# Five small loads put ahead on ScalarE's queue in a linear attention with two MLPs

## The chip, the cores and the metric

One core of a Trainium2 chip runs the whole program. Its engines are TensorE (PE in the profile; its weight loads are PEld), VectorE (DVE), ScalarE (ACT), GpSimd (POOL) and SyncE (SP), which here only issues DMAs. The metric is the device time of one launch in microseconds; the time of a kernel is the median of its runs.

## The reference

Attention without a softmax, an RMS norm over each head, and two MLPs one after the other, all in float32:

```python
kv = np.einsum('bhsd,bhse->bhde', k, v)
out = np.einsum('bhsd,bhde->bhse', q, kv)                    # 4 batches, 8 heads, 576 rows, 64 wide
out = out / np.sqrt(np.mean(out * out, axis=-1, keepdims=True) + 1e-06) * g_norm
x = out.transpose(0, 2, 1, 3).reshape(2304, 512)
h = x @ moe_w_in                                             # 512 -> 2048
x = (np.maximum(h, 0.0) + np.log1p(np.exp(-np.abs(h)))) @ moe_w_out    # softplus, 2048 -> 512
h = x @ moe2_w_in
result = np.maximum(0.01 * h, h) @ moe2_w_out                # leaky ReLU
```

In the kernel q, k, v are 4.7 MB each; the weights are named w1 to w4 and come as 8.4 MB each, since each number is stored in two words.

## The kernel before

The work falls into two stages. In the **attention stage** (about the first 70 us) 16 units of one batch and two heads each go through a pipeline: the sync queue loads q, k and v of a unit (`load`, tiles qa, ka, va, 128 partitions with four rows each; five buffers of each), and once per batch the 64 rows of each head that are left over (qr, kr, vr). The tiles are copied into another order (qp, kp) by ScalarE, VectorE or GpSimd (`copy_to`, line 418 on ScalarE), TensorE transposes q (line 497), multiplies k by v (lines 506 and 511) and q by the result (line 547), VectorE and ScalarE take squares, sums and the norm, and TensorE transposes the normed rows (tile xn, line 632) into xy, which stays on the chip. Beside that, the first weights are loaded (tile mf, line 667) and decoded.

In the **MLP stage** TensorE multiplies in blocks of 128x128 by 384 or 256 columns: line 922 for the first product of an MLP, lines 1179 and 1184 for the second, which read the tile rb. rb is laid over the attention's tiles when these are done with. Intermediate blocks go to a scratch tensor xscr in DRAM and come back.

What stands in which order is settled before the program runs: `Plan` collects the steps, takes the first 500 or so from a list written out by hand (`FIRST`, where S is a load on the sync queue, A ScalarE, D VectorE, P GpSimd, E TensorE) and orders the rest by due times. `keep_warm` (line 476) puts multiplications of idle data on TensorE, 17 calls at the start (`N_WARM`) and a few in between, each of two instructions in the trace. The first thing on ScalarE is the load of its table (line 1395), the last line before `plan.run()`.

A DMA reports its end through one of eight semaphores, named DMAHW0 to DMAHW7, which are handed out in turn over all the DMAs of the program, whichever queue they stand on. A DMA whose semaphore is still in use by the one eight places ahead waits for that one.

Of the kernel before, what the change touches and what calls it, by code (L numbers as in the profile page):

```python
# [168 lines left out]
def linear_attention_two_mlps(  # L169
# [32 lines left out]
    nc = tc.nc  # L202
# [34 lines left out]
    const = ctx.enter_context(tc.tile_pool(name="const", bufs=1))  # L237
# [155 lines left out]
        nc.gpsimd.memset(t_[RL:], 0.0)  # L393
    for t_ in qtl:
        nc.gpsimd.memset(t_[:, RL:2 * RL], 0.0)

    plan = Plan()
    op = plan.op
# [872 lines left out]
    for t in range(2):  # L1271
# [3 lines left out]
                out=graw[t * D:(t + 1) * D, :], in_=g_norm.rearrange("(p o) -> p o", o=1)  # L1275
# [116 lines left out]
                w2_decode(g + 1, no - 4)  # L1392
    with tc.manual_schedule():

        nc.scalar.preload_act_table_set("natural_log_exp_and_others")
        plan.run()

# [31 lines left out]
```

## Time and profile before

| | us |
|---|---|
| median of 3 runs | 779.09 (778.41 to 779.94) |
| the profiled execution | 778.38 |
| its span, from first to last instruction | 776.5 |
| TensorE busy | 770.4 |
| VectorE busy | 676.3 |
| ScalarE busy | 546.4 |

The profile shows one execution. Busy time says how full an engine is, but TensorE's ends are modelled, so a little waiting can hide in it. The chain of waits tells which work ended last at each moment, followed back from the end; "SPq" in it is time in which the sync queue issues a DMA, and "DMA" the time from issue to landing. The windows show busy time, DMA share and GB/s in each stretch, which is where a start-up shows. Times in the trace count from the start of the span.

### The profile page before, as it was taken

The numbers are of one execution on the slowest core, as the hardware profiler recorded it, in microseconds if no ns is written. First come the engines' busy times: TensorE is split into PE (matmuls) and PEld (weight loads), VectorE is DVE, ScalarE is ACT, GpSimd is POOL, SyncE is SP. The second block draws the span as 40 slices with busy tenths as digits, with TensorE's granted clock in tenths as the row PEclk, the third lists the DMA queues.
The fourth block names the chain that finished last, engine by engine and source line by source line (L and its number), as shares of the span: only waits on it lengthen the run. The fifth ranks groups of instructions, "written<-read, shape, count | busy, mean of one in ns | idle before, by whom it ended". The sixth has DMA issues, their size and how long they took to land.

```text
span 776.5 us, 13282 instructions
## 1 busy us (share of the span) xinstructions
PE 770.4 (99%) x5061; PEld 767.0 (99%) x5061; DVE 676.3 (87%) x1079; ACT 546.4 (70%) x936; POOL 20.0 (3%) x36
## 2 busy tenths in 40 slices
PE   9999999999999999999999999999999999999998
PEld 9999999999999999999999999999999999999997
DVE  3999999999899887996899999998799877886667
ACT  4899989886776865863688799977667645554441
POOL 2430000000000000000000000000000000000000
PEclk9999999999999999999999999999999999999999
DMA  9986767694794784683675659786675772562814
GB/s 282 324 290 211 289 235 290 240 336 166 308 336 147 277 343 135 254 310 124 239 290 203 264 202 345 286 306 225 257 274 178 281 252 104 215 240 99 312 42 122
DMA packets 77103, 186.99 MB, mean 241 GB/s; under 512 B 11504, under 2 KB 51440, under 8 KB 77040
## 3 DMA queue, kind: packets, MB, share of 16 engines
q1 hardware_dynamic: 75424, 185.36, 66.6%
q10 hardware_dynamic: 1616, 0.79, 0.4%
q8 instruction: 40, 0.66, 0.3%
q14 instruction: 23, 0.19, 0.1%
HBM read 146.80 MB, written 39.32 MB: 240 GB/s over the span
## 4 chain that ended last, share of the span: by engine, by line
PE 95%; DVE 2%; SPq 1%; ACT 1%; DMA 1%; issue 1%; DVEq 0%; ACTq 0%
PE ps L922 43%; PE ps L1179 23%; PE ps L1184 23%; PE ps L1012 2%; PE ps L547 1%; PE ps L506 1%; DMA ka<-in_k_dram 1%; SPq L447 1%; PE ps L632 1%; DVE ss L573 0%; PE ps L497 0%; PE ps L554 0%; DVE xn L610 0%; ACT sq L568 0%; PE ps L511 0%
## 5 line engine op out<-in xcount | busy, mean ns | idle before, releaser
L922 PE MATMUL ps<-ra 128*128 128x384 f32 x1932 | 386.1, 335 | 0.0
L922 PEld LDWEIGHTS ps<-ra 128*128 128x128 f32 x1932 | 332.1, 188 | 0.0
L1179 PE MATMUL ps<-rb 128*128 128x256 f32 x1512 | 204.4, 282 | 0.0
L1184 PE MATMUL ps<-rb 128*128 128x384 f32 x1008 | 201.2, 334 | 0.0
L1179 PEld LDWEIGHTS ps<-rb 128*128 128x128 f32 x1512 | 198.4, 189 | 0.1
L1184 PEld LDWEIGHTS ps<-rb 128*128 128x128 f32 x1008 | 177.1, 188 | 0.0
L951 ACT ACTIVATE rb<-mf 128x768 fp32r<-128x768 f32 x154 | 130.0, 845 | 63.1 <-PE ps L1179 34.0
L956 DVE TENSOR_TENSOR rb<-mf,rb 128x768 fp32r<-128x768 f32 x154 | 146.5, 952 | 23.4 <-ACT rb L951 22.8
L794 DVE TENSOR_TENSOR xy<-ps,xy 128x384 f32<-128x384 f32 (+2 forms) x247 | 134.4, 548 | 33.8 <-PE ps L1179 22.8
L1036 DVE TENSOR_TENSOR mf<-mf 128x768 f32<-128x768 f32 x68 | 64.2, 951 | 2.4 <-ACT mf L937 1.5
L1229 ACT ACTIVATE mf<-ps 128x384 f32<-128x384 f32 x92 | 44.9, 488 | 29.0 <-PE ps L922 28.5
L1236 DVE TENSOR_TENSOR mf<-ps,mf 128x384 f32<-128x384 f32 x92 | 50.5, 553 | 12.3 <-PE ps L922 8.4
L1241 ACT ACTIVATE ps<-ps 128x384 f32<-128x384 f32 x46 | 22.1, 481 | 20.3 <-PE ps L922 20.1
L937 ACT ACTIVATE mf<-mf 128x768 f32<-128x768 f32 x26 | 21.8, 843 | 15.1 <-DVE mf L1236 14.9
L1098 ACT ACTIVATE rb<-rc 128x512 fp32r<-128x512 f32 x44 | 27.5, 625 | 3.5 <-PE ps L1179 2.7
L1101 DVE TENSOR_TENSOR rb<-rc,rb 128x512 fp32r<-128x512 f32 x44 | 29.8, 682 | 0.2 <-ACT rb L1098 0.2
L943 ACT ACTIVATE mf<-mf 128x768 f32<-128x768 f32 x24 | 20.2, 840 | 11.0 <-DVE mf L1236 11.0
L1195 ACT ACTIVATE ps<-ps 128x384 f32<-128x384 f32 (+2 forms) x44 | 21.1, 480 | 6.3 <-PE ps L1184 3.1
L943 ACT ACTIVATE mf<-ps 128x384 f32<-128x384 f32 x32 | 15.6, 488 | 10.4 <-PE ps L922 10.2
L789 ACT ACTIVATE xy<-ps 128x384 f32<-128x384 f32 (+2 forms) x40 | 19.0, 483 | 3.2 <-PE ps L1179 1.5
L707 ACT ACTIVATE sqr<-mf 128x512 uint16<-128x512 uint16 x26 | 20.4, 784 | 0.0
L825 ACT ACTIVATE ra<-xy 128x768 fp32r<-128x768 f32 x21 | 17.7, 841 | 3.7 <-PE ps L922 3.4
(125 smaller groups left out, 754.9 us busy)
## 6 DMA issues: line engine op xcount, KB each, us to landing
ra<-xscr SPq DMA_DIRECT2D x124, 768.0 KB, 6.2
xscr<-ra SPq DMA_DIRECT2D x37, 768.0 KB, 4.2
mf<-in_moe_w_in_dram SPq DMA_DIRECT2D x18, 512.0 KB, 5.5
mf<-in_moe_w_out_dram SPq DMA_DIRECT2D x18, 512.0 KB, 5.0
lf<-in_moe_w_in_dram SPq DMA_DIRECT2D x14, 512.0 KB, 7.3
lf<-in_moe_w_out_dram SPq DMA_DIRECT2D x14, 512.0 KB, 4.9
ka<-in_k_dram SPq DMA_DIRECT2D x16, 256.0 KB, 5.3
qa<-in_q_dram SPq DMA_DIRECT2D x16, 256.0 KB, 5.4
```

What stands on the lines that cost most here:

```text
L794: {"D": t_d(n)}, lambda e: nc.vector.tensor_tensor(dst, src, dst, ALU.add),
L922: nc.tensor.matmul(o, w_[:, a, c:c + P], e_[:, b, kk, :], start=(not on and which < 2 and kk == 0 and n == 0), stop=(kk == 1 and n == 2), ...
L943: lambda e: nc.scalar.activation(dst(), src(), AF.Prelu, alpha=0.01),
L951: {"A": t_a(n)}, lambda e: nc.scalar.activation(g[:, 0, :, :], c.ap, AF.Copy),
L956: lambda e: nc.vector.tensor_tensor(g[:, 1, :, :], c.ap, g[:, 0, :, :].bitcast(F32), ALU.subtract),
L1036: lambda e: nc.vector.tensor_tensor(to.ap, x.ap, y.ap, ALU.subtract),
L1098: op({"A": t_a(512)}, lambda e: nc.scalar.activation(w_[:, 0], src(), AF.Copy), sk, hk)
L1101: lambda e: nc.vector.tensor_tensor(w_[:, 1], src(), w_[:, 0].bitcast(F32), ALU.subtract), sk + hk, lk,
L1179: nc.tensor.matmul(y[:, 256 * (j % 2):256 * (j % 2 + 1)], G_[:, a, m, js], w_[:, b, m, :], **flags)
L1184: nc.tensor.matmul(y[:, :BN], w_[:, a, m, js], G_[:, b, m, :], **flags)
L1229: {"A": t_a(BN)}, lambda e: nc.scalar.activation(c[:, m, :], src, AF.Copy),
L1236: lambda e: nc.vector.tensor_tensor(c[:, m, :], src, c[:, m, :], ALU.add),
```

## The change

Ahead of all other work of ScalarE, its queue issues five DMAs, one each for q, k, v, w1 and w2. Each fetches 80 single words: from five places, a fifth of the tensor apart, 16 words with 64 bytes between them, one word for each of 16 partitions. They land in five tiles of 16x5 words that nothing reads. The tiles are taken from the pool `const`, ahead of the attention's tiles.

```diff
--- before.py
+++ after.py
@@ -393,6 +393,13 @@
         nc.gpsimd.memset(t_[RL:], 0.0)
     for t_ in qtl:
         nc.gpsimd.memset(t_[:, RL:2 * RL], 0.0)
+
+    first_words = []
+    for t_, name in ((q, "q"), (k, "k"), (v, "v"), (w1, "w1"), (w2, "w2"),):
+        w = t_.rearrange("b h s d -> (b h s d)") if len(t_.shape) == 4 else t_.rearrange("a b -> (a b)")
+        step = w.shape[0] // 5
+        w = w[:5 * step].rearrange("(n m) -> n m", m=step)[:, :256].rearrange("n (r x) -> r n x", x=16)
+        first_words.append((w[:, :, 0:1], const.tile([16, 5, 1], t_.dtype, name="first_" + name)))
 
     plan = Plan()
     op = plan.op
@@ -1392,6 +1399,8 @@
                 w2_decode(g + 1, no - 4)
     with tc.manual_schedule():
 
+        for src, there in first_words:
+            nc.scalar.dma_start(out=there, in_=src)
         nc.scalar.preload_act_table_set("natural_log_exp_and_others")
         plan.run()
 
```

In the built program the other instructions of each engine stand in the order in which they stood; lines after 395 move down by 7, those at the end by 9. This is the start of the sync queue's list before, where `waits` names the semaphores that an instruction waits for, and the number behind a tile's name is that of the buffer:

```order
L447 DMA ka_104<-in_k_dram 128x2x256
L447 DMA qa_98<-in_q_dram 128x2x256
L465 DMA qr_113<-in_q_dram 64x4x64
L447 DMA qa_99<-in_q_dram 128x2x256
L447 DMA va_109<-in_v_dram 128x2x256
L447 DMA ka_103<-in_k_dram 128x2x256
L465 DMA qr_113<-in_q_dram 64x4x64
L458 DMA vr_117<-in_v_dram 64x8x64
L458 DMA kr_115<-in_k_dram 64x8x64 [waits DMAHW0_49]
L447 DMA va_108<-in_v_dram 128x2x256 [waits DMAHW1_49]
L667 DMA mf<-in_moe_w_in_dram 128x4x256 [waits DMAHW2_49]
L1274 DMA graw<-in_g_norm_dram 64x1 [waits DMAHW3_49]
```

and now:

```order
L454 DMA ka_104<-in_k_dram 128x2x256
L454 DMA qa_98<-in_q_dram 128x2x256
L472 DMA qr_113<-in_q_dram 64x4x64
L454 DMA qa_99<-in_q_dram 128x2x256 [waits DMAHW0_49]
L454 DMA va_109<-in_v_dram 128x2x256 [waits DMAHW1_49]
L454 DMA ka_103<-in_k_dram 128x2x256 [waits DMAHW2_49]
L472 DMA qr_113<-in_q_dram 64x4x64 [waits DMAHW3_49]
L465 DMA vr_117<-in_v_dram 64x8x64 [waits DMAHW4_49]
L465 DMA kr_115<-in_k_dram 64x8x64 [waits DMAHW5_49]
L454 DMA va_108<-in_v_dram 128x2x256 [waits DMAHW6_49]
L674 DMA mf<-in_moe_w_in_dram 128x4x256 [waits DMAHW7_49]
L1281 DMA graw<-in_g_norm_dram 64x1 [waits DMAHW0_49]
```

The loads are the same; the first that waits for a semaphore was kr, the ninth, and is now qa, the fourth.

ScalarE's queue before, up to its second wait for a weight or a product:

```order
L1395 ACT_TABLE_LOAD
L418 ACTIVATE qp_120<-qa_99 128x512 [waits DMAHW3_49]
L418 ACTIVATE kp_122<-ka_104 128x512 [waits DMAHW0_49]
L418 ACTIVATE kp_121<-ka_103 128x512 [waits DMAHW5_49]
L418 ACTIVATE qp_119<-qa_98 128x512 [waits DMAHW1_49]
L681 ACTIVATE mf<-mf 128x512 [waits DMAHW2_49]
L568 ACTIVATE sq_132<-ps_89 128x512 [waits PE_49]
```

and now:

```order
L1403 DMA first_q<-in_q_dram 16x5x1
L1403 DMA first_k<-in_k_dram 16x5x1
L1403 DMA first_v<-in_v_dram 16x5x1
L1403 DMA first_w_155<-in_moe_w_in_dram 16x5x1
L1403 DMA first_w_156<-in_moe_w_out_dram 16x5x1
L1404 ACT_TABLE_LOAD
L425 ACTIVATE qp_120<-qa_99 128x512 [waits DMAHW0_49]
L425 ACTIVATE kp_122<-ka_104 128x512 [waits DMAHW1_49]
L425 ACTIVATE kp_121<-ka_103 128x512 [waits DMAHW2_49]
L425 ACTIVATE qp_119<-qa_98 128x512 [waits DMAHW3_49]
L688 ACTIVATE mf<-mf 128x512 [waits DMAHW7_49]
```

Five DMAs stand ahead of the table load, with DMAHW0 to DMAHW4 as their semaphores in this order; the copies wait for the same loads under other numbers.

The five tiles take 32 bytes of each partition apiece, so the attention's tiles and rb start 160 bytes further on.

## Rows read from the trace of the kernel before

**Rows 1.** The page: busy times, and the chain's shares by engine.
```profile
PE 770.4 (99%) x5061; PEld 767.0 (99%) x5061; DVE 676.3 (87%) x1079; ACT 546.4 (70%) x936; POOL 20.0 (3%) x36
...
PE 95%; DVE 2%; SPq 1%; ACT 1%; DMA 1%; issue 1%; DVEq 0%; ACTq 0%
```

**Rows 2.** The chain of waits from 0 to 40 us: start, us, what.
```profile
by line: DMA ka<-in_k_dram 15.2%; SPq L447 12.6%; issue 9.6%; PE ps L547 9.6%; DVE ss L573 5.2%; PE ps L506 4.5%; DVE xn L610 4.4%; SPq L465 3.4%; SPq L458 3.1%; PE ps L497 2.7%; PE ps L554 2.2%; PE ps L632 2.2%; ACT qt L432 1.6%; DVE mf L7
...
0.73 0.45 SPq L447
...
2.50 0.60 SPq L447
...
9.56 0.47 SPq L447
...
10.07 6.09 DMA ka<-in_k_dram
```

**Rows 3.** Windows of the start; the first line names the columns.
```profile
core 0: us, PE busy (x) PEld busy (x) DVE busy (x) ACT busy (x) POOL busy (x), PEclk, DMA share, GB/s
...
4.00:5.00 1.00, 1.00 (x6) 1.00 (x6) 0.00 (x0) 0.00 (x0) 0.00 (x0) 1.00 0.63 165
...
7.00:8.00 1.00, 1.00 (x9) 1.00 (x9) 0.00 (x0) 0.47 (x1) 0.00 (x0) 1.00 1.24 269
8.00:9.00 1.00, 1.00 (x11) 1.00 (x10) 0.00 (x0) 1.00 (x2) 0.00 (x0) 1.00 0.84 231
...
10.00:11.00 1.00, 1.00 (x11) 1.00 (x10) 0.46 (x2) 0.00 (x0) 0.00 (x0) 1.00 1.05 289
...
13.00:14.00 1.00, 1.00 (x11) 1.00 (x10) 0.89 (x3) 0.68 (x2) 0.00 (x0) 1.00 1.02 343
...
15.00:16.00 1.00, 0.78 (x5) 0.47 (x5) 1.00 (x4) 0.60 (x1) 0.67 (x1) 1.00 1.10 386
...
16.00:48.00 32.00, 30.97 (x261) 29.56 (x259) 29.74 (x72) 27.21 (x69) 12.17 (x17) 1.00 1.09 330
```

**Rows 4.** Timeline of the start: start, us, engine, line, operation, count, [idle before <-releaser].
```profile
0.73 1.28 ACT L1395 ACT_TABLE_LOAD   x1 [0.73 <-PEq L1411]
...
1.05 7.01 PE L476 MATMUL ps<-xy 128*128 128x128 f32 x34 [1.05 <-DVE xy L244]
...
6.32 0.63 ACT L418 ACTIVATE qp<-qa 128x512 f32<-128x512 f32 x1 [4.30 <-DMA qa<-in_q_dram]
...
7.90 0.38 PE L497 MATMUL ps<-ident,qp 128*128 128x128 f32 x2
...
14.02 1.06 PE L547 MATMUL ps<-kvm,qt 128*128 128x128 f32 x8
...
15.26 1.13 PE L497 MATMUL ps<-ident,qp 128*128 128x128 f32 x6 [0.18 <-DVE qp L420]
...
16.25 0.63 ACT L418 ACTIVATE kp<-ka 128x512 f32<-128x512 f32 x1 [0.54 <-DMA ka<-in_k_dram]
```

**Rows 5.** By tile: landing of k's first load; stores' issue, landing; g_norm's loads' landing.
```profile
DMA to landing us min/median/max: 2.9/2.9/2.9
...
L1122 ACTq DMA_DIRECT2D out_dram<-xy x5: 379/430/692, 767.7 to 773.3; - x5
...
DMA to landing us min/median/max: 2.0/3.2/8.0
...
DMA to landing us min/median/max: 4.5/5.5/6.4
```

**Rows 6.** Groups by form: count | busy us, mean ns | idle before.
```profile
L1179 PE MATMUL ps<-rb 128*128 128x256 f32 x1512 | 204.4, 282 | 0.0
L1184 PE MATMUL ps<-rb 128*128 128x384 f32 x1008 | 201.2, 334 | 0.0
...
L497 PE MATMUL ps<-ident,qp 128*128 128x128 f32 x64 | 11.7, 276 | 0.5 <-ACT qt L432 0.3 <-DVE qp L420 0.2
...
L632 PE MATMUL ps<-ident,xn 128*128 128x128 f32 x64 | 9.7, 275 | 0.2 <-ACT xy L620 0.2
```

## The prediction

> **What bounds the kernel now.** I read the page first, then the chain of waits in order of time, then the start of the program in the timeline and in one-microsecond windows. On the page TensorE is busy 99% of the span, and the chain that ended last is 95% TensorE; DMA, the sync queue and issue together are 3% of it [rows 1]. So nothing that touches loads can matter where the two MLPs run; the only place where a load ends last is the start. The chain in order of time shows that place exactly: the sync queue issues loads back to back from 0.73 us, the last of that run is k's fifth load (tile ka, buffer ka2), issued at 10.07, it takes 6.09 us to land, and ScalarE's copy of it follows at 16.25 [rows 2, 4]. Behind that the chain doesn't come back to a DMA before 40 us: that one load is 15.2% of these 40 us, and no other stands among the shares [rows 2]. The reader should see two things there: the fourth load (qa, the one that starts at 2.50) is issued without any wait, and each piece of the chain up to 10.07 is only the time to issue.
>
> TensorE in the same stretch is not waiting: it multiplies idle data from 1.05 us, comes to the first real transpose at 7.90, and runs row upon row to 15.08 (14.02 + 1.06); its next row starts at 15.26 after an idle 0.18 us that VectorE's copy of a load released [rows 4]. In windows it is busy throughout up to 15, 0.78 of the microsecond 15 to 16, and 30.97 of the 32 us from 16 to 48 [rows 3]. That gives a ceiling: 0.22 + 1.03 = 1.25 us of idle TensorE is all that better loads could give back by these rows. (The weight loads stand idle longer there, 0.53 + 2.44 = 2.97 us in the same rows, because the end of a matmul is modelled; so the ceiling is 1.25 us, loosely.)
>
> **The change part by part.** ScalarE's queue gets five DMAs of 80 words each ahead of its table load; the sync queue's list is the same as before, and so is the rest of ScalarE's. What differs on the sync queue is what its loads wait for: completions go round eight semaphores (DMAHW0 to 7), the five word DMAs take the first five, and so the fourth to eighth loads now wait for one word DMA each, where before the first wait stood at the ninth. From the ninth load on the wait is for the load eight places back, as it was.
>
> ScalarE itself: five issues at 0.43 us, the median of ScalarE's own store issues, are 2.15 us (3.5 us at their longest, 0.692), so the 1.28 us table load ends at 0.73 + 2.15 + 1.28 = 4.2 us, at worst 5.5 [rows 4, 5]. Its first copy starts at 6.32 after waiting 4.30 us for a load [rows 4]. That wait hides it all: cost 0. Were loads on hand at once, the cost would be about 2 us.
>
> The new waits of the sync queue: the fourth load waits for the words of q. Nothing in the trace is such a DMA, so bounds. Below: the fastest landing of any store, 2.0 us from issue, gives 0.73 + 2.0 = 2.73, against 2.50 before: 0.23 us late. Above: the one tiny load in the trace, g_norm's 0.2 KB, takes 4.5 us at best, behind other loads: 5.23, or 2.73 us late [rows 5]. Nearest is k's first load, which like the words starts on empty queues: 2.9 us, of which moving 256 KB at 343 GB/s is 0.76; the rest, 2.14, gives 2.87, so 0.37 us late [rows 3, 5]. I take 0.37. The four word DMAs behind it leave ScalarE about 0.43 us apart, and the loads that wait for them leave the sync queue 0.47 us or more apart [rows 2], so each is landed when it is asked for and no further wait adds up. Queued behind the waiting load is every other load; all of them move by the 0.37 us, since behind 5 us the DMA engines are full and the lag is not caught up.
>
> The words' own time on the DMA engines: 400 words, 25 on each of 16. In the window 7 to 8, when 256-byte pieces move at 269 GB/s, one piece takes an engine 256 / (269 / 16) = 15 ns [rows 3]; 25 of them are 0.38 us. The lower end is 0, for the engines are only 0.63 busy in the window 4 to 5 [rows 3]. I take 0.10, near the lower end, because the words fall into that gap.
>
> What the words may give: loads run at 165, 231 and 289 GB/s in the windows 4 to 5, 8 to 9 and 10 to 11, against 343 in 13 to 14 [rows 3]. If every dip were the price of a first access to a region, and the words took it away, (178 + 112 + 54) / 343 = 1.0 us would come back. The lower end is 0, and below it is excluded only in so far as the same accesses are made anyhow. What speaks for the low end: k's first load is the first access of all, and it is the fastest, 2.9 us, while g_norm's and others late in the queue take 4.5 and more [rows 5]; and a part of the dip at 4 is merely the sync queue's pace. I take 0.25 us.
>
> A rule of the Trainium skill speaks against the change here: HBM Reference, section Latency, gives an access 0.2 us on average and 2 us at high load, so a slow read would be a matter of load and not of being the first. k's fast first load on empty queues agrees with it (2.9 us), and the dips come when the queues are full; no row separates the two causes. By that rule the gain is 0 and the sum below is 0.25 us higher.
>
> Sum: 0.37 + 0.10 - 0.25 = +0.22 us at k's fifth load, and as that is on the chain, at the end. Span 776.5 + 0.2 = 776.7; with the 1.88 us that lie around it (778.38 - 776.5) the profiled execution would be 778.6. The median of the runs is 0.71 above the profiled one, so 779.09 + 0.2 = **779.3 us**, a change of 0.03%. A measurement of this kernel can tell about 0.2%, or 1.56 us, from no change; this is none.
>
> **The rivals.**
> *The words do what they look meant for.* The dips go (1.0 us earlier) and the wait costs only its lower end (0.23). For it: the dips lie where loads first come to new regions of q, v and the first weights. Against it: TensorE is packed up to 15.08, so a load that lands early there gains nothing, and behind it ScalarE and VectorE take turns on the chain. Net 0.77 us at most of loads, some 0.6 at the end: 778.5. To pass 0.2% it would have to take more than the whole ceiling of 1.25 us.
>
> *The words themselves are slow and hold the sync queue.* The place is the fourth load; the mechanism is the shared semaphores, the price is the landing of a word DMA minus the 2.50 us at which that load goes now. If it is like g_norm's 4.5 us [rows 5], all loads from the fourth on come 2.73 us later, the transposes at 7.90 that had q's copy ready at 6.95 (6.32 + 0.63) run dry, and the end moves by 2.73 + 0.10 - 0.25, about 2.5 us: 781.6. It decides from a landing of about 3.5 us after the first issue on (0.73 + 3.5 - 2.50 + 0.10 - 0.25 = 1.58 us). For it: each word DMA touches five far places with every engine, and five such are in flight together. Against it: the queues are empty then, and 3.5 us is more than a whole 256 KB load took there.
>
> *The tiles move.* Five tiles of 32 bytes lie ahead of the attention's tiles and of rb, so these start 160 bytes later, no longer on a multiple of 64. TensorE reads rb in 405.6 us of its busy time, so 1% slower reads would be 4 us: 783. Against it: in the kernel before the tiles xn already start at such an address, and the transposes that read them take 275 ns, those from qp at an even one 276 [rows 6].
>
> *The change doesn't do what it says*: where the words land late but the sync queue's waits come after them, or the dips stay, the time is the forecast without its gain, 779.55, inside the same class.
>
> **How the numbers follow.** Forecast, with the words landing by 3.2 us and the dips partly or wholly staying: 0.66. The words help: 0.17, of which 0.04 for more than 0.2%, since the ceiling is only loosely 1.25. The words hold the queue: 0.13, of which 0.10 pass 0.2%. The tiles: 0.04, of which 0.03 pass. So faster 0.04, same 0.83, slower 0.13. Range: the lower end is all dips gone against the smallest wait, 779.09 + 0.23 - 1.0 = 778.3; the upper end takes the wait up to the price between the middle and the tiny load's, 779.09 + 1.9 = 781.0. About 0.05 stay out below and 0.10 above.
>
> **What would show it.** Right: in the profile after, the sync queue waits some 0.4 us before its fourth load and not before the fifth to eighth; k's fifth load is issued at about 10.4; ScalarE's first copy starts at about 6.7; the windows behind 4 us move at the same rates; from 48 us on every stretch is as long as before. Wrong: a fourth load at 4 us or later, waits at the fifth to eighth loads too, windows 4 to 12 all near 340 GB/s with k's fifth load landed before 15.5, or matmuls from rb that take other than 334 ns. The forecast would also fail if the first transposes moved by more than the loads did.

## The result, and the profile after

The changed kernel takes 784.76 us (783.93 to 787.81, 6 runs) against 779.14 (778.41 to 779.94, 6 runs): ratio 1.0079, 95% interval 1.0063 to 1.0094, 5.6 us slower where 0.2 was forecast. The profiled execution took 783.93, its span is 782.1.

The page of the changed kernel, busy times and the chain's shares, which answer to [rows 1]; then three of its groups by form (count | busy us, mean ns), of which the last two answer to [rows 6], and the first of the three as it was before. Line numbers there are 7 higher.

```profile
PE 774.0 (99%) x5061; PEld 770.5 (99%) x5061; DVE 677.3 (87%) x1079; ACT 546.7 (70%) x936; POOL 20.7 (3%) x36
...
PE 96%; DMA 3%; SPq 1%; issue 0%; ACTq 0%; DVE 0%
```

```profile
L929 PE MATMUL ps<-ra 128*128 128x384 f32 x1932 | 388.8, 336 | 0.0
L1186 PE MATMUL ps<-rb 128*128 128x256 f32 x1512 | 204.8, 282 | 0.0
L1191 PE MATMUL ps<-rb 128*128 128x384 f32 x1008 | 202.4, 335 | 0.0
```

```profile
L922 PE MATMUL ps<-ra 128*128 128x384 f32 x1932 | 386.1, 335 | 0.0
```

TensorE's busy time went up by 3.6 us for the same 5061 instructions. So most of the loss is not waiting at the start: the same matmuls took longer, far behind it. The largest part, 2.7 us, stands at line 929, which reads only ra, a tile that did not move; the lines that read rb took 1.2 and 0.4 us more.

The start, in the order of [rows 2 to 4]. The sync queue's waits up to 6 us (who waited for what: us in all, times, longest):

```profile
SPq L454 <- DMA first_q<-in_q_dram: 1.0, 1, 1.0
```

The chain of waits, 0 to 40 us (start, us, what):

```profile
1.24 3.17 DMA first_k<-in_k_dram
...
4.43 0.41 SPq L454
...
9.77 5.84 DMA qa<-in_q_dram
...
15.62 7.39 DMA kr<-in_k_dram
...
23.02 3.64 DMA ka<-in_k_dram
```

The timeline (start, us, engine, line, operation, [idle before]):

```profile
3.23 1.28 ACT L1404 ACT_TABLE_LOAD   x1 [3.23 <-issue]
3.44 0.37 SPq L454 DMA_DIRECT2D qa<-in_q_dram  x1
...
3.86 0.47 SPq L454 DMA_DIRECT2D va<-in_v_dram  x1
4.43 0.41 SPq L454 DMA_DIRECT2D ka<-in_k_dram  x1
...
6.32 0.63 ACT L425 ACTIVATE qp<-qa 128x512 f32<-128x512 f32 x1 [1.81 <-DMA qa<-in_q_dram]
...
10.96 0.46 PE L518 MATMUL ps<-vr,kr 128*128 128x128 f32 x2 [0.88 <-DMA kr<-in_k_dram]
...
24.85 1.13 PE L513 MATMUL ps<-va,kp 128*128 128x128 f32 x8 [1.38 <-DMA va<-in_v_dram]
```

Windows (PE, PEld, DVE, ACT, POOL busy, clock, DMA share, GB/s):

```profile
4.00:5.00 1.00, 1.00 (x6) 1.00 (x6) 0.00 (x0) 0.51 (x1) 0.00 (x0) 1.00 0.46 100
8.00:9.00 1.00, 1.00 (x11) 1.00 (x10) 0.00 (x0) 0.87 (x2) 0.00 (x0) 1.00 1.16 213
10.00:11.00 1.00, 0.12 (x2) 0.07 (x1) 0.00 (x0) 0.00 (x0) 0.00 (x0) 1.00 1.07 354
16.00:48.00 32.00, 30.15 (x253) 28.83 (x254) 29.32 (x70) 26.31 (x67) 11.66 (x16) 1.00 1.11 296
```

The fourth load goes at 3.44 instead of 2.50, held by the words of q. ScalarE's table load ends at 4.5 and costs nothing: the first copy, which reads that fourth load, still starts at 6.32, so the late load landed as early as before. But TensorE waits 0.88 us for the left-over rows of k at 10.96, which it didn't before, and 1.38 us for v's at 24.85. The chain now stays with loads until 26.66. And from 16 to 48 us the loads run at 296 GB/s instead of 330 [rows 3], with the DMA engines as full (1.11 against 1.09): a full engine moves less.

One statement ahead of the prediction is wrong and bears on these waits: that the five word DMAs have DMAHW0 to DMAHW4. The lists there show it, for the copies of ka_104 and qa_98 wait for DMAHW1 and DMAHW3, which are thus the semaphores of k's and q's first loads. In the built program the DMAs of the two queues are mixed in the order of the semaphores, and the words have 0, 2, 4, 5 and 7. So it is the fourth, sixth, eighth, ninth and eleventh loads that wait for a word; the fifth and the seventh wait for the first loads of k and of q.

How long the matmuls of the MLP stage take from start to start is seen best in the timeline of TensorE (start, us, line, operation, tiles, count), where groups of six alternate between lines 922 and 1184 (929 and 1191 in the changed kernel). Before, and then after:

```profile
199.77 1.20 PE L1184 MATMUL ps<-rb 128*128 128x384 f32 x6
...
225.77 1.03 PE L922 MATMUL ps<-ra 128*128 128x384 f32 x5
```

```profile
199.73 1.21 PE L1191 MATMUL ps<-rb 128*128 128x384 f32 x6
...
225.90 0.86 PE L929 MATMUL ps<-ra 128*128 128x384 f32 x4
```

Between the two rows of each fence lie 25 groups. They took 225.77 - 199.77 = 26.00 us before, 1.040 each, and 225.90 - 199.73 = 26.17 after, 1.047 each. The same in counts of matmuls that start between 200 and 400 us, before and after:

```profile
200.00:400.00 200.00, 200.00 (x1156) 1.00 0.66 242
```

```profile
200.00:400.00 200.00, 200.00 (x1149) 1.00 0.65 238
```

That is 0.61% fewer, at full granted clock (1.00) in both. A steady loss of that size from about 84 us, where line 922 begins, cannot come from a load at the start. The first row of that line, before and then after, gives a length for the MLP stage, counted from there to the end of the span:

```profile
84.33 4.32 PE L922 MATMUL ps<-ra 128*128 128x384 f32 x24
```

```profile
85.69 4.32 PE L929 MATMUL ps<-ra 128*128 128x384 f32 x24
```

It is 776.5 - 84.3 = 692.2 us before and 782.1 - 85.7 = 696.4 after: 4.2 of the 5.6 us that the span grew by.

### The profile page after: what moved, and what is told of

It reads as the page before. It is cut to its first block, busy times and chain, and to the rows that moved or that the text cites. A ratio compares the mean times of both kernels' runs of the same rounds, so it can differ in the third digit from the quotient of the medians.

```text
span 782.1 us, 13287 instructions
## 1 busy us (share of the span) xinstructions
PE 774.0 (99%) x5061; PEld 770.5 (99%) x5061; DVE 677.3 (87%) x1079; ACT 546.7 (70%) x936; POOL 20.7 (3%) x36
## 4 chain that ended last, share of the span: by engine, by line
PE 96%; DMA 3%; SPq 1%; issue 0%; ACTq 0%; DVE 0%
PE ps L929 43%; PE ps L1186 23%; PE ps L1191 22%; PE ps L1019 2%; PE ps L554 1%; PE ps L513 1%; DMA kr<-in_k_dram 1%; PE ps L639 1%; DMA qa<-in_q_dram 1%; PE ps L504 1%; DMA ka<-in_k_dram 0%; DMA first_k<-in_k_dram 0%; PE ps L518 0%; PE ps L561 0%; SPq L454 0%; SPq L465 0%
## 5 line engine op out<-in xcount | busy, mean ns | idle before, releaser
L1236 ACT ACTIVATE mf<-ps 128x384 f32<-128x384 f32 x92 | 44.9, 488 | 29.6 <-PE ps L929 29.2
L950 ACT ACTIVATE mf<-ps 128x384 f32<-128x384 f32 x32 | 15.6, 488 | 10.7 <-PE ps L929 10.4
L944 ACT ACTIVATE mf<-ps 128x384 f32<-128x384 f32 x32 | 15.5, 486 | 6.9 <-PE ps L929 6.8
```

Source lines behind the costliest of these rows:

```text
L944: {"A": t_a(n)}, lambda e: nc.scalar.activation(dst(), src(), AF.Softplus),
L950: lambda e: nc.scalar.activation(dst(), src(), AF.Prelu, alpha=0.01),
L1236: {"A": t_a(BN)}, lambda e: nc.scalar.activation(c[:, m, :], src, AF.Copy),
```

## Experiments

Two theories stood against each other. **W**: the word DMAs cost the time, by their waits and what follows. **P**: the addresses cost it, since the five word tiles push the attention's tiles and rb 160 bytes on. All experiments are made from the kernel before or the changed one; "before" is about 778.9 in each comparison. The bytes by which tiles move are counted in each partition. The last column is the MLP stage in the one profiled execution of each kernel, counted as above (692.2 us before); it leaves the start out, which differs by 1 us and more from profile to profile (rb_160, whose start is unchanged, comes to line 922 at 85.3 us against 84.3).

| kernel | words | load tiles moved by | rb moved by | median us | ratio to before (95%) | MLP stage us |
|---|---|---|---|---|---|---|
| changed | q k v w1 w2 | 160 | 160 | 784.76 | 1.0079 (1.0063 to 1.0094) | 696.4 |
| place_160 | none | 160 | 160 | 783.79 | 1.0059 (1.0046 to 1.0071) | 695.8 |
| words_256 | q k v w1 w2 | 256 | 256 | 780.26 | 1.0020 (1.0012 to 1.0029) | 692.8 |
| att_160 | none | 160 | 0 | 779.34 | 1.0009 (1.0000 to 1.0017) | 692.1 |
| rb_160 | none | 0 | 160 | 783.01 | 1.0048 (1.0034 to 1.0062) | 696.2 |
| place_256 | none | 256 | 256 | 779.05 | 1.0001 (0.9992 to 1.0010) | 692.2 |
| words_qkv_256 | q k v | 256 | 256 | 779.00 | 1.0002 (0.9993 to 1.0011) | 692.4 |
| words_w_256 | w1 w2 | 256 | 256 | 779.01 | 1.0000 (0.9991 to 1.0009) | 692.3 |
| rb_32 | none | 0 | 32 | 783.24 | 1.0054 (1.0040 to 1.0068) | 696.8 |
| rb_64 | none | 0 | 64 | 788.39 | 1.0125 (1.0111 to 1.0139) | 701.9 |
| rb_128 | none | 0 | 128 | 781.06 | 1.0026 (1.0016 to 1.0035) | 694.3 |
| all_160 | none | 160 | 160, and ra too | 780.33 | 1.0019 (1.0008 to 1.0031) | 692.1 |
| after_rb_back | q k v w1 w2 | 160 | 256 | 781.55 | 1.0029 (1.0019 to 1.0038) | 692.5 |

**place_160: the tiles without the words.**

```diff
+    spare = const.tile([P, 40], F32, name="spare")
     plan = Plan()
```

> No word is asked for; one unread tile of 160 bytes stands where the five word tiles stood, so the attention's tiles and rb start 160 bytes later, as in the changed kernel. Theory P (the addresses cost the time): about 783.5 us, the MLP stage 3.7 us longer as in the changed kernel, and the loads from 16 us on as slow as there; only the 0.9 us by which the first loads came late are missing. Theory W (the word DMAs cost the time, through the waits of the sync queue and what follows from them): 779.1, as before.

It lost 0.59%, of the 0.79% that the changed kernel lost. So the words are the smaller part, and the greater part comes of memory that nothing reads or writes. Theory W falls as the main cause.

**words_256: the words without the odd addresses.**

```diff
+        first_words.append((w[:, :, 0:1], const.tile([16, 5, 1], t_.dtype, name="first_" + name)))
+    spare = const.tile([P, 24], F32, name="spare")
```

> The five word DMAs as in the changed kernel, and 96 bytes more behind their tiles, so that the attention's tiles and rb start 256 bytes later. Theory P: 779.6 to 780.0 (before, plus the late fourth load: 0.9 us at k's fifth load in the changed kernel), with gaps between matmuls as before. Theory W: 784.5 as in the changed kernel, with the MLP stage 3.7 us longer.

It lost 0.20%, somewhat more than P expected. Its sync queue is held as in the changed kernel; the fourth load in its timeline:

```profile
3.51 0.39 SPq L455 DMA_DIRECT2D qa<-in_q_dram  x1
```

**att_160 and rb_160: one place at a time.** In the first the spare tile stands at the head of the attention's pool, which rb doesn't share; in the second at the head of rb's own.

```diff
     attp = att.__enter__()
+    spare = attp.tile([P, 40], F32, name="spare")
```
```diff
-        buf(ctx.enter_context(tc.tile_pool(name="wm", bufs=1, reuse_waits="tile")), "rb", F32R)
+        wm = ctx.enter_context(tc.tile_pool(name="wm", bufs=1, reuse_waits="tile"))
+        wm.tile([P, 40], F32, name="spare")
+        buf(wm, "rb", F32R)
```

> No words; only the attention's tiles start 160 bytes later, rb stands where it stood. Theory P, with two parts (load tiles: slower loads from 16 us on; rb: slower changes between matmuls): 779.5 to 780.5, gaps between matmuls of the MLP stage as before, GB/s of 16 to 48 us near 295 instead of 330. If the load tiles' addresses don't matter: 779.1 and 330 GB/s. Theory W: 779.1.

> No words; only rb starts 160 bytes later, the attention's tiles stand where they stood. Theory P with two parts: 782.8 (779.1 + 3.7), the start as before, the first matmul of each six at 180 ns instead of 173 for line 922. Theory W: 779.1.

rb alone loses 0.48%, the load tiles alone 0.09%, whose interval just reaches no change. The groups of six in rb_160's timeline of TensorE, and its count of matmuls from 200 to 400 us:

```profile
200.40 1.21 PE L922 MATMUL ps<-ra 128*128 128x384 f32 x6
...
225.52 1.21 PE L922 MATMUL ps<-ra 128*128 128x384 f32 x6
```

```profile
200.00:400.00 200.00, 200.00 (x1149) 1.00 0.65 239
```

24 groups in 25.12 us, 1.047 each, and 1149 matmuls: both are the changed kernel's numbers to the last digit. The load tiles show in the windows from 16 to 48 us instead, att_160 first, then place_256, where the same tiles stand on a multiple of 256 again:

```profile
16.00:48.00 32.00, 30.41 (x257) 29.00 (x256) 29.86 (x71) 26.40 (x66) 11.17 (x16) 1.00 1.10 295
```

```profile
16.00:48.00 32.00, 30.95 (x258) 29.31 (x257) 29.93 (x72) 26.97 (x69) 12.55 (x17) 1.00 1.07 318
```

295 GB/s against 318 (before: 330, changed: 296), though in att_160 neither a word nor a wait was added. The other profiles fall the same way: 286 to 296 in the five kernels whose load tiles moved by 160 bytes, 313 to 330 in the nine others.

What TensorE waited for in att_160 (who waited for what: us in all, times, longest) shows the changed kernel's two waits for loads, with no word in the program:

```profile
PE ps L507 <- DMA va<-in_v_dram: 1.0, 1, 1.0
PE ps L512 <- DMA kr<-in_k_dram: 0.7, 1, 0.7
```

So those two waits can't be put down to the hold alone.

**place_256: the move alone, in a whole step of 256 bytes.** The spare tile of place_160 with 64 words instead of 40.

> No words; one unread tile of 256 bytes, so the attention's tiles and rb start 256 bytes later. The counterpart of words_256. If what words_256 lost (1.29 us, ratio 1.0020) came of the word DMAs, this is 779.0 as before; if moving the tiles costs something by itself even in whole steps of 256 bytes, it is 779.5 to 780.3.

No cost that the interval shows. So what words_256 lost is the words' doing.

**words_qkv_256 and words_w_256: fewer words, no hold.** The list of tensors in the loop is cut to three or to the last two, and the spare tile filled up to 256 bytes.

```diff
-    for t_, name in ((q, "q"), (k, "k"), (v, "v"), (w1, "w1"), (w2, "w2"),):
+    for t_, name in ((q, "q"), (k, "k"), (v, "v")):
```

> The words of q, k and v alone (those of w1 and w2 are left out), tiles 256 bytes later as in words_256. With three words the first load that waits for a word is the sixth, at 3.65 us, when the words of q (3.42 in the changed kernel) have landed. Theory H (what the words cost is the hold of the sync queue at the fourth load, 1.0 us): 779.0, and the fourth load goes at 2.50. Theory D (the words disturb the loads on the DMA engines themselves): about 3/5 of 1.29 us, 779.7 to 779.8. Were the first accesses worth something, it would be under 779.0.

> The words of w1 and w2 alone (those of q, k and v are left out), tiles 256 bytes later. The first load that waits for a word is the seventh, at 4.17 us, long after the words landed. Theory H (the hold of the sync queue at the fourth load is what all five words cost): 779.0. If the words of the two weight tensors cost something themselves, since five far places of 8.4 MB tensors are read: 779.6 to 780.2.

Both are equal to before, and to place_256. With three words or two the semaphores come out so that the fourth load waits for nothing; words_qkv_256's timeline of the sync queue, fourth to sixth load:

```profile
2.51 0.59 SPq L455 DMA_DIRECT2D qa<-in_q_dram  x1
3.15 0.47 SPq L455 DMA_DIRECT2D va<-in_v_dram  x1
3.67 0.47 SPq L455 DMA_DIRECT2D ka<-in_k_dram  x1
```

So two or three word DMAs cost nothing that the intervals show (at most 0.11%), and 0.2% is the price of five of them, the only number at which the fourth load is held. That fits H; five words without the hold were not run. The other half of the answer stands here too: no gain from the first accesses shows. Its windows:

```profile
4.00:5.00 1.00, 1.00 (x6) 1.00 (x6) 0.00 (x0) 0.00 (x0) 0.00 (x0) 1.00 0.53 128
8.00:9.00 1.00, 1.00 (x12) 1.00 (x10) 0.00 (x0) 0.50 (x1) 0.00 (x0) 1.00 1.10 228
10.00:11.00 1.00, 1.00 (x10) 0.88 (x9) 0.23 (x2) 0.00 (x0) 0.00 (x0) 1.00 1.10 354
```

The dips at 4 and at 8 are there as before (128 and 228 GB/s; before 165 and 231). The one at 10 is gone, but so it is without any word in rb_32 (362 GB/s) and rb_160 (323).

**rb_32, rb_64, rb_128: what about the address.** As rb_160, with a spare tile of 8, 16 and 32 words.

> Only rb moves, by 32 bytes. 160 is 32 more than a multiple of 128. If what counts is whether rb's address is a multiple of 64: as rb_160, 783.0, line 922's first of six at 180 ns. If it is the distance of 160 bytes as such: another time.

> Only rb moves, by 64 bytes. If a multiple of 64 is enough: 779.0, all gaps between matmuls at 173 to 174 ns. If it takes a multiple of 128 or 256: as rb_160, 783.0.

> Only rb moves, by 128 bytes. Moves by 32, 64 and 160 cost 4.4, 9.5 and 4.0 us, by 256 nothing. If the cost goes by the address within 256 bytes: between 779.5 and 790, and not 779.0. If a multiple of 128 is enough: 779.0, gaps as before.

rb_32 took the expected time, but not by the expected way: from 200 to 400 us line 922's first of six takes 170 to 174 ns there, not 180, and later ones up to 185. The expectation for rb_64 was wrong both ways: a multiple of 64 is not enough, and it is the worst of all, 1.25%. In its timeline of TensorE 23 groups take 24.22 us, 1.053 each:

```profile
200.69 1.21 PE L922 MATMUL ps<-ra 128*128 128x384 f32 x6
...
224.91 1.22 PE L1184 MATMUL ps<-rb 128*128 128x384 f32 x6
```

Half of 256 is not enough either. 256 was free in place_256, words_qkv_256 and words_w_256.

**all_160: rb at rb_160's address, but ra moved with it.**

```diff
+    spare = const.tile([P, 40], F32, name="spare")
     buf(const, "ra", F32R)
```

> No words. One unread tile of 160 bytes ahead of ra, so that ra, mf, the attention's tiles and rb all start 160 bytes later and keep their distances. Theory R (it is the distance between ra and rb, from which TensorE reads by turns): the gaps between matmuls are those of before, and the time 779.0 plus up to 0.5 for the load tiles. Theory S (it is rb's own address): 783 or more, and with ra moved too more than rb_160.

Its groups of six, and its count from 200 to 400 us:

```profile
199.91 1.20 PE L923 MATMUL ps<-ra 128*128 128x384 f32 x6
...
225.91 0.85 PE L1185 MATMUL ps<-rb 128*128 128x384 f32 x4
```

```profile
200.00:400.00 200.00, 200.00 (x1156) 1.00 0.66 242
```

25 groups in 26.00 us, 1156 matmuls: as before, with rb at the very address at which rb_160 was slow. So at 160 bytes it is not rb's own address that counts (theory S falls) but how it stands to what moved with it. That was ra, from which TensorE reads in the groups between, and also mf, which TensorE doesn't read here. That it is ra is argued from single starts: in rb_160, from 200 to 400 us, each of 96 groups from ra has 180 ns between its first two starts (173 before), and each of 95 from rb has 176 or 177 at its first and 175 or 176 at its last gap, to 1 ns. A clash with the traffic of other engines would hardly repeat so exactly.

The 0.19% that is left was expected at up to 0.5 us and is 1.5. Its MLP stage is as long as before (692.1), so by its profile it lies at the start; its loads, those of mf among them, run at 292 GB/s from 16 to 48 us, much as in att_160. Why it is more than att_160's 0.09% is not shown; the two intervals overlap.

**after_rb_back: the changed kernel with rb alone put right.** The edit of rb_160, in the changed kernel, with 24 words.

> The changed kernel with 96 unread bytes ahead of rb alone, so that rb stands 256 bytes from its old place, while the words and the attention's tiles are as in the changed kernel. Theory R: what is left is the hold (1.2 us) and the load tiles (0.4 us), 780.5, and the gaps between matmuls of the MLP stage are those of before. If the 4 us of rb_160 and the words' cost depended on each other: over 782.

```profile
200.00:400.00 200.00, 200.00 (x1156) 1.00 0.66 242
```

The gaps of the MLP stage are back to before's. The time is 1 us over the expectation but adds up in ratios: words_256's 0.20% and att_160's 0.09% are 0.29%, and 0.29% was measured (each within about 0.1%).

## Why the prediction was wrong

The sum of the parts, as measured each by itself: rb 0.48%, the hold by the words 0.20%, the load tiles 0.09%, together 0.77% of the changed kernel's 0.79%. By the prediction's own steps:

- **What bounds the kernel**: read rightly for the kernel before. TensorE's matmuls are the chain, and loads end last only at the start. This should have turned the attention to whatever the change touches in the matmuls; it turned it to the loads.
- **The tiles move**: this is the step that failed. The sum has no term for it; the rival that named it was the answer, and was put at a chance of 0.04. Measured alone, rb's move costs 3.7 us (rb_160, 1.0048). That the rival's price was 4 us is luck: it took 1% slower reads of rb, a figure that no row gives, while most of the loss stands at line 929, which reads ra. What was wrong is the evidence against it, mean durations of two transposes [rows 6]. Each of these reads ident and one other tile, not two tiles by turns in long groups, and a mean of modelled durations hardly shows the loss even where it is known to be there (335 against 334 ns for the 384-column ones from rb); the start-to-start times do. TensorE reads ra and rb by turns, and in the kernel before these stand a multiple of 256 bytes apart (ra, mf and sqr between them take 70, 23 and 2 KB of a partition), so that its trace could not show what another distance costs. A bound from 0 to 4 us belonged into the range, which ended at 781.0.
- **The mechanism** named there, slower reads from an address that isn't a multiple of 64, was wrong too: rb_64, where rb stands on a multiple of 64, is slower than rb_160, and all_160 is not slow in the MLP stage.
- **The load tiles** had no term at all. The DMAs that fill them write rows of 1 KB and 256 bytes, and in the built program these no longer start on a multiple of 256. Median landings of k, v and q from 16 to 48 us (count, KB each, median us), before, then after:

```profile
ka<-in_k_dram SPq DMA_DIRECT2D x10, 256.0 KB, 5.1
va<-in_v_dram SPq DMA_DIRECT2D x10, 256.0 KB, 5.4
qa<-in_q_dram SPq DMA_DIRECT2D x10, 256.0 KB, 5.4
```

```profile
ka<-in_k_dram SPq DMA_DIRECT2D x9, 256.0 KB, 6.2
va<-in_v_dram SPq DMA_DIRECT2D x9, 256.0 KB, 6.4
qa<-in_q_dram SPq DMA_DIRECT2D x9, 256.0 KB, 6.4
```

  About a microsecond more each, in a stretch where DMA engines are full; without a word, in att_160, the medians are 6.5. They spread, though: in rb_160, whose load tiles didn't move, they are 5.5 to 6.2. Why only 0.09% of this reached the end in att_160 is not shown. The Trainium skill (DMA: Bandwidth & Descriptors, How a descriptor splits into AXI transactions) says that a transaction has to start at a multiple of 256 bytes, so that a descriptor which starts elsewhere fetches bytes that it doesn't use; it speaks of reads. The trace agrees in the direction, with the written side moved, 286 to 296 GB/s against 313 to 330; the transactions themselves no run here shows.
- **The new wait**: the right place and the right mechanism, the size off. It was put at 0.37 us from k's first load; the words of q took 2.7 us to land, not 2.14, so it is 3.44 - 2.50 = 0.94 us:

```profile
L1403 ACTq DMA_DIRECT2D first_q<-in_q_dram x1: 462/462/462, 0.7 to 0.7; - x1
...
DMA to landing us min/median/max: 2.7/2.7/2.7
```

  The loads that wait for words were misread (above), but that the later word DMAs add hardly any wait was right: one wait stands in the list above, and the sixth load starts just behind the words of k (1.24 + 3.17 = 4.41), some 0.06 us late. That all loads move by the hold was not: the fourth, forecast to bring the first copy to 6.7, landed as early as before, and k's fifth load was issued at 10.84 instead of 10.07 (forecast: 10.4). That the lag reaches the end was right in kind: words_256 lost 0.20%, 0.9 to 2.3 us by its interval, which holds the 0.94.
- **The words' gain**: put at 0.25 us with 1.0 as the upper end. No gain shows in words_qkv_256 and words_w_256 (ratios 1.0002 and 1.0000): 1.0 us is outside their intervals, but 0.25 can't be told from 0. The Trainium skill's figures for an access (HBM Reference, Latency), from which the prediction argued that slow reads go with load and not with a first access, are not contradicted: the dips at 4 and 8 stayed. No run here shows what makes them.
- **ScalarE's queue**: free, as said; its wait of 4.30 us became 1.81.

What stays open: why a distance that is off costs what it does. The five distances give 4.2, 9.7, 2.0 and 3.7 us for 32, 64, 128 and 160 bytes, by the ratios, and 0 for 256, with no order in them that I could name; that it goes by the distance within 256 bytes is the plainest reading, not shown for other multiples, and that rb's own address plays no part is shown for 160 alone. The order also changes with the shapes: from 200 to 400 us rb_32 does fewer matmuls than rb_64 (1139 against 1141, before 1156), from 400 to 600, where most groups from rb have 256 columns, more (1370 against 1351, before 1378).

Nor is it only the change from one tile to the other that costs. From 200 to 400 us, at 160 bytes, the extra time stands at the first and last gaps of a six. At 64 bytes it runs through the six, and the longest gap of the groups from rb, 185 ns, is the fourth, where both reads (weights and columns) are from rb. Which of TensorE's two reads is held up, nothing here separates.

## What to carry to other kernels

A small tile that nothing reads is not free if it stands ahead of others: it moves them, and both loads and matmuls that read two tiles by turns can depend on where these lie. Put small tiles last, or pad them to 256 bytes, which cost nothing here, and before a small change is judged by what it does, compare the addresses in the built program. A DMA on an idle queue isn't free either where completion semaphores go round all queues: count which loads come to wait for it.

## What the runs showed of the hardware

- Matmuls that read by turns from two tiles got slower where the tiles' distance was 32, 64, 128 or 160 bytes past a multiple of 256, with TensorE busy throughout at its full granted clock (1.00) from 200 to 400 us. At 64 the kernel lost 1.25%, and a group of six took 1.053 us on average instead of 1.040. It shows in start-to-start times and in counts per stretch, hardly in mean durations.
- From 16 to 48 us, with the DMA engines full, loads ran at 286 to 296 GB/s into tiles 160 bytes past a multiple of 256, and at 313 to 330 into tiles on one (five and nine kernels, one profile each).
- A DMA of 80 words took 2.7 to 3.2 us to land at the start of the program, about as long as k's first load of 256 KB in the kernel before (2.9 us).
